# Crossing the quadrants of softmax maxima and sums on VectorE in four more attention units (123 to 126)

## The chip, the cores and the metric

The kernel runs on one core of a Trainium2 chip. The metric is the device time of one execution in microseconds. The core's engines each work through a list of instructions of their own, in order: PE (TensorE, matrix products; PEld is its weight load), DVE (VectorE), ACT (ScalarE), POOL (GpSimd) and SP (SyncE, which here issues most DMAs). They meet only through semaphores. The matrix products write to a memory called PSUM, everything else lies in SBUF; both have 128 partitions, and a quadrant is a group of 32 of them.

## What is computed

A transformer block on 2048 rows of width 576: a layer norm with a shift and scale made from a conditioning vector, attention with 32 query heads over the last 512 rows of a cache of 16 key/value heads, a gated residual, a second layer norm, and a gated MLP of width 4608 with a ReLU on the gate.

```python
W = min(4096, max(256, Sk // 4))                       # 512
q = (x @ wq).reshape(B, Sq, Hq, Dh).transpose(0, 2, 1, 3)
k = jnp.repeat(k_cache[:, :, Sk - W:, :], rep, axis=1)
v = jnp.repeat(v_cache[:, :, Sk - W:, :], rep, axis=1)
p = softmax(einsum("bhqd,bhkd->bhqk", q, k) * Dh ** -0.5)
o = einsum("bhqk,bhkd->bhqd", p, v)
return o.transpose(0, 2, 1, 3).reshape(B, Sq, Hq * Dh) @ wo
...
h = _layernorm(x) * (1 + ca) + sa
x = x + ga * A(h)
h = _layernorm(x) * (1 + cb) + sb
x = x + gb * B(h)                                      # B: (relu(h @ W_gate) * (h @ W_up)) @ W_down
```

## The kernel before

All products take their operands split in two, a rounded high part and the remainder as a low part, and three of the four partial products are summed (high by high, high by low, low by high). So nearly every tile is rounded on ACT (`hi`), and POOL or DVE subtracts to get the rest (`lo`).

Attention runs in 128 units. A unit is one query head on 512 of the 2048 rows; `UNITS` lists them. In unit u the code at the bottom of the listing issues, engine by engine and in this order:

- PE: the scores of u (`s_half` twice, L496 to L498, keys on the partitions, rows along the free axis), the query projection of u+1 (`qproj`, L424), in some units `spread` (L530), a piece of the output projection (`wo_piece`, L660), the first and second half of the product with the values for u-1 (`pv_half`, L633 to L635), another piece. The third product of each score group needs `qlo` of its unit, which DVE made in the unit before (L480).
- DVE: the maximum over the scores in blocks of 32 partitions (L501), the maximum over the four key blocks (`max_pre`), the sums of unit u-1 over blocks of 32 partitions (`sum_pre`, L522), the crossing (below), the broadcast of the maximum (`mb`, L571), the subtraction of the maximum from both halves of the scores (L591), the reciprocal of the sums (L547) and its broadcast (L552), `qlo` of u+1 (L480), the first addition of the key sum (L606), the multiplication of the values' product of u-1 by the reciprocals (L641).
- ACT: the rounding of the query (L476), copies that carry the output projection (L669, L693), the exponentials of the two halves (L593) and their roundings (`hi_half`, L577).
- POOL: two more additions of the key sum (`ksum_op`, L609), then the low parts of both halves (`lo_half`, L600), and the low part of the attention output (L649).

The crossing. After L501 and L522 every partition holds the maximum, or the sum, of its own quadrant; the result over all keys needs the four quadrants together. There are three forms:

- Units 4 to 107, `by_moves`: DVE alone. `cross` copies partitions 64 to 127 beside 0 to 63 and 32 to 63 beside 0 to 31 (`move`, L534, on a small tile), reduces four values to one for maxima and sums (L542), and moves the result back to the other quadrants (L534 twice). Then the reciprocal reads SBUF, later in the unit.
- Units 108 to 126: DVE writes the maxima masked by quadrant (L516), PE multiplies by a matrix of ones and zeros (`spread`, L530, into the PSUM tile `qm`), and DVE reduces what comes back (L558) and takes the reciprocal there and then.
- Units 0 to 3 and 127, `by_pe`: the same crossing through PE, and PE also subtracts the maximum from the scores (L587) with the broadcast maximum that ACT has rounded (`mr`, L569).

`late_hi` is the same test as `by_moves`: where it holds, ACT does both exponentials and then both roundings, otherwise it rounds the first half before the second exponential.

The last units carry work for the MLP besides. Its first matrix product is done with seven products for eight block products, on sums and differences of blocks of the normalized rows. Those are made here: `h0_comb` adds two 128x512 tiles on DVE (L886), `h0_cut` rounds one on ACT (L893) and gets the low part on POOL (L906), or on DVE for 32 partitions of the third tile (L908). A table of times `10 * unit + place` sets where each stands; DVE runs them at the end of a unit, behind L641. L606, L886 and L908 read two tiles in SBUF, L591, L641 and L480 one in PSUM and one in SBUF.

Of the kernel before, what the change touches and what calls it, by code (L numbers as in the profile page):

```python
# [27 lines left out]
CFG = {'a0': (('s', 'vvp', 'vvv'), ('m', 'aap', 'avp'), ('w', 'aav')), 'a1': (('w', 'aap', 'vap'), ('m', 'vvp', 'vvv'), ('s', 'avp'))}  # L28
PE0, PE1, MLP0 = 4, 1, 8
NLAST = 5  # L30
MOVES = 108


@with_exitstack
def kernel(
# [467 lines left out]
                                axis=AX.X, op=ALU.max, apply_transpose=True)  # L503

    def by_moves(u):
        return PE0 <= u < MOVES

    def max_pre(u):
        m = t5[u][:, 0:4, :].rearrange("p k b -> p b k")
        if by_moves(u):  # L510
            nc.vector.tensor_reduce(t5[u][:, 4, :], m, axis=AX.X, op=ALU.max)
            return
        bps[u] = psM.tile([P, 512], F32, tag="mm", name=f"qm{u}")
        t = bps[u][:, 128:144]
        nc.vector.tensor_reduce(t, m, axis=AX.X, op=ALU.max)
        nc.vector.tensor_tensor(t5[u][:, 4:8, :], mask[:, :, None].to_broadcast([P, 4, 16]),  # L516
                                t[:, None, :].to_broadcast([P, 4, 16]), op=ALU.mult)

    def sum_pre(u):
        if u + 1 == NU:  # L520
            t5[NU] = sp.tile([P, 12, 16], F32, tag="t5", name=f"t5_{NU}", bufs=1)
        nc.vector.tensor_reduce(t5[u + 1][:, 5 if by_moves(u + 1) else 8, :],  # L522
                                ks_.pop(u).rearrange("p (b j) -> p b j", j=32),
                                axis=AX.X, op=ALU.add, apply_transpose=True)
# [21 lines left out]
    def sum_inv(u):  # L546
        nc.vector.reciprocal(t5[u + 1][:, 1, :], t5[u + 1][:, 1, :] if by_moves(u + 1) else bps[u + 1][:, 64:80])  # L547
# [1226 lines left out]
```

## Time and profile before

| | us |
|---|---|
| median of 3 runs (2859.11 to 2862.62) | 2862.01 |
| profiled execution | 2857.6 |
| its span | 2855.8 |
| units 108 to 127, from the first score maximum of 108 to the last exponential's input of 127 | 1345.7 to 1588.7 |

The first row counts for comparisons; the breakdown comes from one profiled execution. In the rows of the trace the first number is the start in microseconds from the start of the span, the second the time taken, then engine, line, operation, output and inputs with shapes, and how many instructions were merged. In brackets stands how long the engine had been idle and which engine's instruction released it. A row of merged instructions covers them together. A start to the next start can be a little shorter than the time taken, since an instruction's end overlaps the next one's begin. For the stretches, each row gives start and end, length, busy time of PE, PEld, DVE, ACT and POOL with the number of instructions, the granted TensorE clock as a share of full speed, the share of time the DMA engines were busy, and GB/s.

### The profile page before, as it was taken

To read this page: it belongs to the slowest core of one execution; us is meant where nothing else is said; L and a number is where in the kernel's file an instruction comes from. 1 tells how busy PE (TensorE), PEld (TensorE's weight loads), DVE (VectorE), ACT (ScalarE), POOL (GpSimd) and SP (SyncE) were. 2 spreads that over 40 slices of the span, in tenths; PEclk is the share of its full clock that TensorE was granted. 3 is DMA by queue.
4 is the path that set the end of the run, shared out by engine and by line. 5 is a ranking of instruction groups with operands and counts; after the bars stand their busy time and mean duration, and the time that the engine had idled before them with its cause. 6 is when DMAs were issued, how large, how long until landed. Compare 5 with 4: busy or idle time off the path is not lost.

```text
span 2855.8 us, 41174 instructions
## 1 busy us (share of the span) xinstructions
PE 2815.0 (99%) x15006; PEld 2449.5 (86%) x15006; DVE 2246.8 (79%) x3384; ACT 1476.7 (52%) x2105; POOL 2123.8 (74%) x1564
## 2 busy tenths in 40 slices
PE   6999999999999999999999999999999999999999
PEld 5788888888888888888888888888888888888888
DVE  7899999999889998888889756676677466666666
ACT  5766666666766666666656444444444122222221
POOL 5688888888899989877778766788777356656653
PEclk9999999999999999999999999999999999999999
DMA  4012132222232213312243456666667844444442
GB/s 163 24 45 79 65 106 85 83 82 100 95 104 94 92 62 131 105 70 80 68 155 139 150 213 229 231 240 231 234 234 261 338 165 154 155 155 159 159 154 106
DMA packets 164506, 399.57 MB, mean 140 GB/s; under 512 B 15056, under 2 KB 62160, under 8 KB 164304
## 3 DMA queue, kind: packets, MB, share of 16 engines
q1 hardware_dynamic: 132912, 284.69, 29.9%
q10 hardware_dynamic: 31392, 112.26, 10.0%
q8 instruction: 118, 1.93, 0.3%
q14 instruction: 84, 0.69, 0.1%
HBM read 271.16 MB, written 154.57 MB: 149 GB/s over the span
## 4 chain that ended last, share of the span: by engine, by line
PE 83%; DVE 6%; POOL 5%; issue 2%; ACT 2%; DMA 2%; SPq 0%; ACTq 0%; DVEq 0%; POOLq 0%
PE gu L1016 26%; PE wo L660 12%; PE qps L424 11%; PE md L660 8%; PE st_P L1118 6%; PE s L498 3%; PE s L497 3%; PE s L496 3%; PE pv L635 3%; PE pv L634 3%; PE pv L633 3%; POOL lo L600 2%; DVE t L501 1%; DVE p L591 1%; POOL wop L795 1%
## 5 line engine op out<-in xcount | busy, mean ns | idle before, releaser
L600 POOL TENSOR_TENSOR lo<-p,hi 128x1024 fp32r<-128x1024 f32 x256 | 610.6, 2406 | 1.1 <-ACT hi L577 1.1
L609 POOL TENSOR_TENSOR ks<-ks,p 128x512 f32<-128x512 f32 x256 | 351.7, 1374 | 238.7 <-DVE ks L606 135.5
L501 DVE TRANSPOSE_TENSOR_REDUCE t<-s 128x32 f32<-128x1024 f32 x256 | 313.8, 1239 | 85.9 <-PE s L498 76.6
L1016 PE MATMUL gu<-hop_B,wop 128*128 128x512 f32 x1512 | 375.0, 391 | 0.2 <-POOL wop L795 0.2
L1016 PEld LDWEIGHTS gu<-hop_B,wop 128*128 128x128 f32 x1512 | 274.9, 188 | 51.1 <-POOL wop L795 0.9
L1016 PE MATMUL gu<-hop_T,wop 128*128 128x512 f32 x1260 | 316.1, 391 | 0.0
L424 PE MATMUL qps<-hTa,wA 128*128 128x512 f32 x1288 | 312.9, 394 | 3.1 <-DVE hTa L372 1.6
L660 PE MATMUL wo<-woga,ohi 128*128 128x288 f32 x1472 | 298.8, 295 | 2.0 <-POOL woga L183 1.4
L591 DVE TENSOR_TENSOR p<-s,mb 128x1024 f32<-128x1024 f32 x246 | 290.3, 1219 | 4.2
L424 PEld LDWEIGHTS qps<-hTa,wA 128*128 128x128 f32 x1288 | 244.5, 190 | 56.6 <-DVE hTa L372 3.2
L476 ACT ACTIVATE qhi<-qps 128x512 fp32r<-128x512 f32 x128 | 76.4, 597 | 366.9 <-PE qps L424 358.4
L660 PEld LDWEIGHTS wo<-woga,ohi 128*128 128x128 f32 x1472 | 245.9, 188 | 18.8 <-POOL woga L183 3.4
L1016 PEld LDWEIGHTS gu<-hop_T,wop 128*128 128x128 f32 x1260 | 227.8, 188 | 39.0
L577 ACT CAST hi<-p 128x1024 fp32r<-128x1024 f32 x256 | 259.5, 1042 | 1.5
L660 PE MATMUL md<-wogb,hhi 128*128 128x288 f32 x1272 | 256.9, 295 | 0.4 <-DVE acc L671 0.4
L593 ACT ACTIVATE p<-p 128x1024 f32<-128x1024 f32 x246 | 249.5, 1051 | 13.7 <-DVE p L591 13.4
L671 DVE TENSOR_TENSOR acc<-md,acc 128x576 f32<-128x576 f32 x159 | 119.9, 755 | 160.4 <-PE md L660 159.8
L660 PEld LDWEIGHTS md<-wogb,hhi 128*128 128x128 f32 x1272 | 210.9, 188 | 12.6 <-DVE acc L671 1.4
L1127 DVE TENSOR_TENSOR acc<-st_P,acc 128x576 f32<-128x576 f32 x160 | 121.1, 757 | 127.9 <-PE st_P L1118 127.9
L660 PE MATMUL wo<-woga,olo 128*128 128x288 f32 x736 | 217.8, 296 | 1.3 <-POOL olo L649 1.2
L660 PE MATMUL md<-wogb,hlo 128*128 128x288 f32 x636 | 187.5, 295 | 0.0
L649 POOL TENSOR_TENSOR olo<-rb,ohi 128x512 fp32r<-128x512 f32 x128 | 167.4, 1308 | 15.2 <-ACT ohi L645 15.0
(283 smaller groups left out, 7095.3 us busy)
## 6 DMA issues: line engine op xcount, KB each, us to landing
wop<-wk_P SPq DMA_DIRECT2D x133, 640.0 KB
wk_P<-wop ACTq DMA_DIRECT2D x119, 640.0 KB
wr<-wlay SPq DMA_DIRECT2D x68, 384.0 KB
rogb<-wd SPq DMA_DIRECT2D x68, 288.0 KB
againq<-akq SPq DMA_DIRECT2D x18, 640.0 KB
rwA<-wq SPq DMA_DIRECT2D x32, 320.0 KB
wlay<-wg SPq DMA_DIRECT2D x36, 256.0 KB
roga<-wo SPq DMA_DIRECT2D x32, 288.0 KB
```

The source lines that it names most:

```text
L424: return [lambda i=i, a=a, b=b: nc.tensor.matmul(ps, a, b, start=(i == 0), stop=(i == n - 1)) for i, (a, b) in enumerate(ops)]
L501: nc.vector.tensor_reduce(t5[u][:, 2 * h:2 * h + 2, :].rearrange("p k b -> p (k b)"), t.rearrange("p k (b j) -> p (k b) j", j=32), axis=AX ...
L577: nc.scalar.copy(hi_[u, h], pt[u, h])
L591: nc.vector.tensor_tensor(p, t, bc[u][:, None, :].to_broadcast([P, 2, 512]), op=ALU.subtract)
L593: nc.scalar.activation(p, p, AF.Exp, bias=0.0, scale=1.0)
L600: nc.gpsimd.tensor_sub(lo_[u, h], pt[u, h], hi_[u, h].bitcast(F32))
L609: nc.gpsimd.tensor_tensor(ks_[u], ks_[u], p[:, j, :], op=ALU.add)
L649: nc.gpsimd.tensor_sub(olo[u], o.pop(u), ohi[u].bitcast(F32))
L660: nc.tensor.matmul(ps[:, half, :H2], a[:, sl], w[b][:, cs], start=(n == 0 and seed is None), stop=(n == 5), skip_group_check=seed is not None)
L1016: nc.tensor.matmul(ps, a, c, start=s not in heir(m) and i == 0 and s not in seeds_of(m), stop=i == len(ops) - 1, skip_group_check=True)
L1118: nc.tensor.matmul(ps[:, j, :H2], x[:, sl], w[:, y, :], start=n == 0 and not second, stop=n == 2, skip_group_check=True)
L1127: nc.vector.tensor_tensor(t, ps[:, :, :H2], t, op=ALU.add)
```

## The change

The number that ended the range of units crossed by moves becomes a list of units, and 123 to 126 join it. Unit 122 and those before it down to 108 still cross through PE, and so does 127.

```diff
-MOVES = 108
+MOVES = (*range(4, 108), *range(123, 127))
...
     def by_moves(u):
-        return PE0 <= u < MOVES
+        return u in MOVES
```

DVE's list in unit 123 before, from the maximum over the key blocks to the broadcast of the reciprocals (`t_123` is the small tile of maxima and sums, `qm` the PSUM tile that PE's spread writes):

```order
L515 TENSOR_REDUCE qm_16102<-t_123_16092 128x16
L516 TENSOR_TENSOR t_123_16092<-mask,qm_16102 128x64
L522 TENSOR_REDUCE t_123_16092<-ks_16046 128x16
L558 TENSOR_REDUCE t_123_16092<-qm_16102 128x16
L547 RECIPROCAL t_123_16092<-qm_16102 128x16
L571 STREAM_TRANSPOSE mb_16128<-t_123_16092 128x512
L591 TENSOR_TENSOR p_0_16158<-s_0_16085,mb_16128 128x1024
L591 TENSOR_TENSOR p_1_16163<-s_1_16094,mb_16128 128x1024
L552 STREAM_TRANSPOSE rb_16166<-t_123_16092 128x512
```

The same place in the changed kernel:

```order
L511 TENSOR_REDUCE t_123_16092<-t_123_16092 128x16
L522 TENSOR_REDUCE t_123_16092<-ks_16046 128x16
L534 TENSOR_REDUCE t_123_16092<-t_123_16092 64x32
L534 TENSOR_REDUCE t_123_16092<-t_123_16092 32x64
L542 TENSOR_REDUCE t_123_16092<-t_123_16092 32x16 x2
L534 TENSOR_REDUCE t_123_16092<-t_123_16092 32x32
L534 TENSOR_REDUCE t_123_16092<-t_123_16092 64x32
L571 STREAM_TRANSPOSE mb_16110<-t_123_16092 128x512
L591 TENSOR_TENSOR p_0_16159<-s_0_16085,mb_16110 128x1024
L591 TENSOR_TENSOR p_1_16162<-s_1_16094,mb_16110 128x1024
L547 RECIPROCAL t_123_16092<-t_123_16092 128x16
L552 STREAM_TRANSPOSE rb_16168<-t_123_16092 128x512
```

The mask and the reading back of `qm` are gone, four moves and two reductions have come, and the reciprocal has gone behind the subtractions. On PE the instruction L530 is gone from the place between the query projection and the piece of the output projection, and PSUM's `qm` tile with it; the tiles `qps` and `pv` share two banks in turn, without a third in between.

ACT's list in unit 123 before, from the copy that starts a piece of the output projection to the copy that ends it (`p` is a half of the exponentials, `hi` its rounding):

```order
L693 COPY wo_0_16156<-acc_129 128x2x288
L593 ACTIVATE p_0_16158<-p_0_16158 128x1024
L577 CAST hi_0_16161<-p_0_16158 128x1024
L593 ACTIVATE p_1_16163<-p_1_16163 128x1024
L577 CAST hi_1_16201<-p_1_16163 128x1024
L669 COPY acc_129<-wo_0_16156 128x576
```

And in the changed kernel:

```order
L693 COPY wo_0_16157<-acc_129 128x2x288
L593 ACTIVATE p_0_16159<-p_0_16159 128x1024
L593 ACTIVATE p_1_16162<-p_1_16162 128x1024
L577 CAST hi_0_16165<-p_0_16159 128x1024
L577 CAST hi_1_16203<-p_1_16162 128x1024
L669 COPY acc_129<-wo_0_16157 128x576
```

The second exponential has gone ahead of the first rounding; nothing else moved on ACT. Units 124 to 126 change in the same way. POOL's list and the DMAs of SP keep their order.

## The prediction

> **What bounds the kernel now.** I read the page first, then the stretches of the end of the attention stage, then the instructions of each engine in order of time there.
>
> ```profile
> span 2855.8 us, 41174 instructions
> PE 2815.0 (99%) x15006; PEld 2449.5 (86%) x15006; DVE 2246.8 (79%) x3384; ACT 1476.7 (52%) x2105; POOL 2123.8 (74%) x1564
> PE 83%; DVE 6%; POOL 5%; issue 2%; ACT 2%; DMA 2%; SPq 0%; ACTq 0%; DVEq 0%; POOLq 0%
> ```
>
> Over the whole span PE is the bound. The change touches units 123 to 126 alone, so the stage there counts:
>
> ```profile
> 1297.30:1309.10 11.80, 11.80 (x63) 10.27 (x63) 10.28 (x18) 7.41 (x11) 8.52 (x6) 1.00 0.14 50
> 1533.50:1545.70 12.20, 12.20 (x66) 10.53 (x65) 11.48 (x17) 8.90 (x13) 10.36 (x7) 1.00 0.46 162
> 1545.70:1557.80 12.10, 12.10 (x65) 10.30 (x64) 11.46 (x17) 7.58 (x11) 10.28 (x7) 1.00 0.52 178
> 1582.10:1594.00 11.90, 10.77 (x59) 8.65 (x59) 7.57 (x15) 6.32 (x9) 8.51 (x5) 1.00 0.44 138
> 1590.00:2856.00 1266.00, 1260.99 (x6942) 1111.16 (x6941) 820.51 (x966) 424.47 (x660) 814.44 (x743) 1.00 0.56 199
> ```
>
> Columns: stretch, length, busy time of PE, PEld, DVE, ACT, POOL, then the clock. The first row is a unit that already crosses by moves: DVE has 1.5 us free. The next two are units 123 and 124: DVE is busy 11.5 of 12.1 to 12.2 us, as full as PE. The fourth is unit 127, the fifth everything behind: PE idles 5 us in 1266, so a delay that PE has at 1590 stays.
>
> DVE from the last third of unit 123 to the start of unit 125, with the starts of units 123, 126 and 127 (L501 opens each unit):
>
> ```profile
> 1533.54 2.37 DVE L501 TRANSPOSE_TENSOR_REDUCE t<-s 128x32 f32<-128x1024 f32 x2
> ...
> 1541.55 0.65 DVE L480 SCALAR_TENSOR_TENSOR qlo<-qps,qhi 128x512 fp32r<-128x512 f32 x1
> 1542.12 0.67 DVE L606 TENSOR_TENSOR ks<-p 128x512 f32<-128x512 f32 x1
> ...
> 1543.43 0.68 DVE L908 TENSOR_TENSOR hy_T<-h,hy_T 32x512 fp32r<-32x512 f32 x1
> 1544.14 1.68 DVE L886 TENSOR_TENSOR lfb<-lfb,lfb 128x512 f32<-128x512 f32 x1
> 1545.74 2.37 DVE L501 TRANSPOSE_TENSOR_REDUCE t<-s 128x32 f32<-128x1024 f32 x2
> 1548.14 0.27 DVE L515 TENSOR_REDUCE qm<-t 128x16 f32<-128x64 f32 x1
> ...
> 1549.84 0.23 DVE L558 TENSOR_REDUCE t<-qm 128x16 f32<-128x64 f32 x1 [0.54 <-PE qm L530]
> ...
> 1550.14 0.67 DVE L571 STREAM_TRANSPOSE mb<-t 128x512 f32<-128x512 f32 x1
> ...
> 1554.32 0.67 DVE L606 TENSOR_TENSOR ks<-p 128x512 f32<-128x512 f32 x1
> ...
> 1555.51 0.68 DVE L886 TENSOR_TENSOR lfb<-lfb,lfb 128x512 f32<-128x512 f32 x1
> 1556.11 1.79 DVE L886 TENSOR_TENSOR h<-h,h 128x512 f32<-128x512 f32 x1
> 1557.82 2.37 DVE L501 TRANSPOSE_TENSOR_REDUCE t<-s 128x32 f32<-128x1024 f32 x2
> ...
> 1570.03 2.37 DVE L501 TRANSPOSE_TENSOR_REDUCE t<-s 128x32 f32<-128x1024 f32 x2
> ...
> 1582.11 2.37 DVE L501 TRANSPOSE_TENSOR_REDUCE t<-s 128x32 f32<-128x1024 f32 x2
> ```
>
> No L501 here waits for PE: each follows the instruction before it at once. The only wait is the 0.54 us of the round trip through PE's spread. So DVE's own chain sets when each unit begins, and lengthening it delays the next. The start of 124 lies 12.20 us behind that of 123, the start of 125 12.08 behind that; 12.21 and 12.08 follow.
>
> **The change, part by part.** First the crossing. The price of moves on DVE is in a unit before 108:
>
> ```profile
> 1311.79 0.27 DVE L511 TENSOR_REDUCE t<-t 128x16 f32<-128x64 f32 x1
> ...
> 1314.05 0.71 DVE L571 STREAM_TRANSPOSE mb<-t 128x512 f32<-128x512 f32 x1
> ...
> 1317.07 0.24 DVE L547 RECIPROCAL t<-t 128x16 f32<-128x16 f32 x1
> ...
> 1318.56 0.67 DVE L606 TENSOR_TENSOR ks<-p 128x512 f32<-128x512 f32 x1
> ```
>
> From the first maximum to the broadcast moves take 1314.05 - 1311.79 = 2.26 us; the spread takes 1550.14 - 1548.14 = 2.00, its wait included. From there to the key sum L606 moves take another 4.51, the spread 4.18: the reciprocal now stands alone. Together 6.77 against 6.18, so +0.59 us of DVE per unit, 4 x 0.59 = +2.36. PE loses one spread per unit:
>
> ```profile
> 1549.36 0.44 PE L530 MATMUL qm<-t,quad 128*128 128x80 f32 x2
> 1549.60 0.51 PE L660 MATMUL wo<-againo,ohi 128*128 128x288 f32 x2
> ```
>
> Start to start 0.24 us, four times 0.96. It counts only where PE is the bound.
>
> Second, the exponentials. POOL's two additions to the key sum (L609) need the second exponential and DVE's L606. Rows of POOL in units 123 and 124 (spread) and, last, behind the L606 of 1318.56 (moves):
>
> ```profile
> 1543.76 1.50 POOL L609 TENSOR_TENSOR ks<-ks,p 128x512 f32<-128x512 f32 x1 [1.76 <-ACT p L593]
> 1545.35 1.62 POOL L609 TENSOR_TENSOR ks<-ks,p 128x512 f32<-128x512 f32 x1
> ```
> ```profile
> 1555.95 3.10 POOL L609 TENSOR_TENSOR ks<-ks,p 128x512 f32<-128x512 f32 x2 [1.74 <-ACT p L593]
> ```
> ```profile
> 1319.37 2.65 POOL L609 TENSOR_TENSOR ks<-ks,p 128x512 f32<-128x512 f32 x2 [2.65 <-DVE ks L606]
> ```
>
> Today POOL starts 1.64 and 1.63 us behind L606, held by ACT. With both exponentials first it starts 1319.37 - 1318.56 = 0.81 us behind, held by DVE. That is nothing by itself, but L908 and L886 follow on DVE 1.2 to 1.3 us behind L606, and the rows show that they suffer from POOL. In unit 124 the first L886, begun 0.44 us ahead of POOL, takes 0.60 start to start; the second, begun 0.16 behind POOL's start, takes 1.71. In unit 123 the L886 begun 0.38 behind takes 1.60, L908 ahead of POOL 0.71. The blocked instruction lasts until the POOL instruction ends and some 0.5 us more (1543.76 + 1.50 = 1545.26, and DVE is free at 1545.74, 0.48 later); in return POOL's second addition needs 1.62.
>
> In the changed kernel POOL is 0.8 us nearer, so the first of the pair falls behind POOL's start in every unit and is blocked too, and the second meets POOL's second addition. DVE is then free 0.48 us behind the end of that addition: (1545.35 + 1.62 - 1543.76) + 0.48 = 3.69 us behind POOL's start, so 0.81 + 3.69 = 4.50 behind L606. Now it is 1545.74 - 1542.12 = 3.62 in unit 123 and 1557.82 - 1554.32 = 3.50 in 124; 125 and 126 repeat 123 and 124 in what they run, and in their length (12.21 and 12.08 us). Cost 2 x 0.88 + 2 x 1.00 = +3.76.
>
> The Trainium skill's page "SBUF — State Buffer", section "Who interferes with whom", says that a VectorE instruction with two SBUF inputs and a GpSimd instruction that reads SBUF lock each other out whole, the one that issued second waiting. The trace agrees in kind (0.68 against 1.68 us for the same L886). By that rule alone the blocked instruction would need only the rest of POOL's addition plus its own 0.60; with 2.65 / 2 = 1.33 for an addition I estimate 1.33 - 0.38 + 0.60 = 1.55 where the row has 1.60, which would take 0.2 off the sum. I take the row.
>
> Sum on DVE at the start of unit 127: 2.36 + 3.76 = +6.1 us. Does PE feel all of it? Unit 127 still crosses through PE:
>
> ```profile
> 1586.44 0.23 DVE L558 TENSOR_REDUCE qm<-qm 128x16 f32<-128x64 f32 x1 [0.78 <-PE qm L530]
> ```
> ```profile
> 1587.98 0.62 ACT L569 CAST mr<-mb 128x512 fp32r<-128x512 f32 x1 [5.52 <-DVE mb L566]
> ```
> ```profile
> 1588.66 1.19 PE L587 MATMUL s<-mr,minus 128*128 128x512 f32 x4
> ```
>
> PE's L587 starts 0.06 us behind the end of ACT's cast, which waits for DVE: PE follows DVE there one for one. One thing gives back: L558 waited 0.78 here where the round trip needs 0.54, since PE was the later one; PE will now be early, -0.24. PE's savings of 0.96 and today's idle 1.13 in this unit vanish in the longer wait. So +6.1 - 0.24 = +5.9 us at L587, and nothing behind gives it back. Ahead of it PE stalls on the low part of q:
>
> ```profile
> 1543.90 0.40 PE L498 MATMUL s<-qlo,againk 128*128 128x512 f32 x1
> ```
>
> Its slack is 1543.90 - (1541.55 + 0.65) = 1.70 us. DVE's lag there is 0.59 in unit 123, then 2.06, 3.65 and 5.12, while PE is faster by 0.24 a unit: the slack is gone in unit 124.
>
> The casts of the first half move about 1 us back on ACT; POOL's L600, which reads them, starts only after both additions, so they cost nothing. Queues: no DMA is added, and those that SP issues behind L908's store move by at most the lag, ahead of their use in the next stage.
>
> The profiled execution took 2857.6 us, its span 2855.8; the median of the runs shown is 2862.0, 4.4 above. The difference goes on the median: 2862.0 + 5.9 = 2867.9, which is 0.21%. What a measurement of this kernel can tell from no change is about 0.2%, 5.7 us, so the forecast sits on that border.
>
> **Rivals.**
>
> A, the forecast: both instructions blocked in each unit. With prices off by some 0.6 us and the runs' own scatter it gives 2865.5 to 2870.
>
> B, only one blocked: when the first is done, DVE takes the second ahead of POOL's waiting addition. Then DVE is free 1.98 + 0.60 = 2.58 us behind POOL's start, 3.39 behind L606: 0.23 and 0.11 less than now, -0.68 in four units, and 2.36 - 0.68 - 0.24 = +1.4, so 2863.4. Against it: POOL's second row starts at 1545.35 while the blocked L886 still runs, so it is already in line. It decides at the end of the first blocked instruction.
>
> C, the other side: DVE's lag is swallowed. PE is the bound, saves 0.96, and POOL starts the sums of unit 126 9.99 instead of 10.22 us behind L501, so PE's 1.13 wait shrinks by 0.23: -1.2, 2860.8. It decides at a lag of 1.70 us at qlo; it needs less than 0.4 us per unit, and the crossing alone is 0.59.
>
> D, PE's clock drops in the new gaps. The largest is in unit 127: PE comes to its spread 5.12 - 1.70 = 3.4 us late, DVE's input 6.1 - 0.24 = 5.9 late, so PE idles 2.5. The row of 1582.10 shows clock 1.00 through a gap of 1.13. Only the start of the program shows a lower one:
>
> ```profile
> 0.00:60.00 60.00, 37.80 (x147) 30.11 (x148) 45.23 (x100) 28.01 (x43) 29.75 (x33) 0.94 0.54 193
> ```
>
> There 22 us of idle time cost at most 0.06 x 60 = 3.6 us. As an upper end: +9.5, 2871.5. The Trainium skill's page "TensorE: Matmul & The Clock Gate", Part 1, has the clock halve after an idle window of about 3.4 us; by that rule a gap of 2.5 would be safe and D would not come.
>
> **How the numbers follow.** A 0.80, split by the border 5.7 below its middle of 5.9: 0.48 slower, 0.32 same. D 0.08, slower. B 0.07, same. C 0.05, same but for 0.01 faster by scatter. Slower 0.56, same 0.43, faster 0.01. The range 2863 to 2871 holds A, B and most of D; A's own is 2865.5 to 2870.
>
> **What would show it.** Right: in units 124 to 126 L501 starts 13.7 us apart on DVE; POOL's L609 0.81 us behind L606, released by DVE; L908 and both L886 above 1.2 us; PE waiting for qlo from unit 125 on, and L587 near 1594.6. Wrong: the first of each pair still at 0.7 us (the lock is not what I read), units 12.7 us apart or less, or PE without a wait for qlo (the lag was covered).

## The result, and the profile after

The changed kernel takes 2868.61 us (median of 7 runs, 2863.92 to 2872.21). The kernel before, on the same chip, takes 2859.11 (7 runs, 2855.87 to 2862.62). The ratio is 1.0031 with a 95% interval of 1.0022 to 1.0040: slower by 9.5 us, and between 6.3 and 11.4. The profiled execution took 2863.92 us, the shortest of the seven, and its span stands 6.3 us above that of the kernel before.

The page's head, and the same stretches as were read of before (length, busy time of PE, PEld, DVE, ACT, POOL, then PE's clock, DMA share, GB/s):

```profile
span 2862.1 us, 41170 instructions
...
PE 2814.9 (98%) x14998; PEld 2449.1 (86%) x14998; DVE 2251.5 (79%) x3400; ACT 1477.4 (52%) x2105; POOL 2124.9 (74%) x1564
```
```profile
1560.20:1573.60 13.40, 12.10 (x63) 10.07 (x62) 13.04 (x21) 8.83 (x12) 9.30 (x6) 1.00 0.30 103
...
1587.10:1599.00 11.90, 9.55 (x41) 7.36 (x40) 7.62 (x15) 5.92 (x8) 7.12 (x4) 0.86 0.41 127
```

The first row is unit 125: it now lasts 13.47 us, and PE is busy for only 12.10 of 13.40, since it waits for DVE. The second is unit 127, and there the clock is 0.86, which was 1.00 before. From 1595 to 2862 PE is busy for 1261.86 of 1267.00 us, so it idles 5.1 us there, about as before.

DVE at the start of unit 123, through unit 124 and to the starts of 125 and 127, and POOL's key sum of unit 124 (the idle time before an instruction and what ended it stand in brackets):

```profile
1533.23 2.37 DVE L501 TRANSPOSE_TENSOR_REDUCE t<-s 128x32 f32<-128x1024 f32 x2
...
1555.87 0.67 DVE L606 TENSOR_TENSOR ks<-p 128x512 f32<-128x512 f32 x1
...
1557.07 1.47 DVE L886 TENSOR_TENSOR lfb<-lfb,lfb 128x512 f32<-128x512 f32 x1
1558.46 1.77 DVE L886 TENSOR_TENSOR h<-h,h 128x512 f32<-128x512 f32 x1
1560.15 2.37 DVE L501 TRANSPOSE_TENSOR_REDUCE t<-s 128x32 f32<-128x1024 f32 x2
1562.56 0.26 DVE L511 TENSOR_REDUCE t<-t 128x16 f32<-128x64 f32 x1
...
1569.33 0.67 DVE L606 TENSOR_TENSOR ks<-p 128x512 f32<-128x512 f32 x1
...
1587.08 2.37 DVE L501 TRANSPOSE_TENSOR_REDUCE t<-s 128x32 f32<-128x1024 f32 x2
```
```profile
1556.69 2.99 POOL L609 TENSOR_TENSOR ks<-ks,p 128x512 f32<-128x512 f32 x2 [2.79 <-DVE ks L606]
```

POOL starts 0.82 us behind L606, released by DVE. Both L886 are blocked, 1.39 and 1.69 us from start to start, and DVE is at the next L501 4.28 us behind L606 where it took 3.50 in this unit before.

PE in units 125 and 127, and the first L1016, a product of the MLP:

```profile
1569.46 0.50 PE L498 MATMUL s<-qlo,againk 128*128 128x512 f32 x1 [1.30 <-DVE qlo L480]
...
1590.67 0.45 PE L530 MATMUL qm<-t,quad 128*128 128x80 f32 x2 [1.33 <-DVE t L522]
1591.78 0.73 PE L619 MATMUL pv<-lo,againv 128*128 128x512 f32 x2 [0.16 <-POOL lo L600]
1593.37 2.07 PE L587 MATMUL s<-mr,minus 128*128 128x512 f32 x4 [0.86 <-ACT mr L569]
1597.55 1.77 PE L1016 MATMUL gu<-hop_B,wop 128*128 128x512 f32 x7
```

L587's four products take 2.07 us instead of 1.19. Stretches around them show why; the clock is the third number from the end:

```profile
1590.00:1593.00 3.00, 1.68 (x6) 0.82 (x6) 2.03 (x6) 0.30 (x1) 1.73 (x1) 1.00 0.40 124
1593.00:1594.00 1.00, 0.63 (x2) 0.53 (x3) 0.65 (x1) 1.00 (x3) 0.08 (x1) 0.71 0.78 267
1594.00:1595.00 1.00, 1.00 (x4) 0.81 (x3) 0.07 (x1) 0.69 (x2) 1.00 (x1) 0.50 0.17 65
```

PE ran at half its clock from about 1593.4 to 1596.8, 3.4 us, behind the three small gaps of unit 127.

Where the 6.3 us are, in PE's and DVE's own times: unit 123 began 0.31 earlier (1533.23 against 1533.54), its start to that of unit 127 took 53.85 instead of 48.57 (+5.28), from there to L587 6.29 instead of 6.55 (-0.26), from L587 to the first L1016 4.18 instead of 2.94 (+1.24), and +0.35 behind it. In the kernel before, whose L587 started at 1588.66, that L1016 stands at:

```profile
1591.60 1.77 PE L1016 MATMUL gu<-hop_B,wop 128*128 128x512 f32 x7
```

### The profile page after: what moved, and what is told of

It is laid out like the page before. It is cut to its first block, busy times and chain, and to the rows that moved or that the text cites. A ratio compares the mean times of both kernels' runs of the same rounds, so it can differ in the third digit from the quotient of the medians.

```text
span 2862.1 us, 41170 instructions
## 1 busy us (share of the span) xinstructions
PE 2814.9 (98%) x14998; PEld 2449.1 (86%) x14998; DVE 2251.5 (79%) x3400; ACT 1477.4 (52%) x2105; POOL 2124.9 (74%) x1564
## 5 line engine op out<-in xcount | busy, mean ns | idle before, releaser
L600 POOL TENSOR_TENSOR lo<-p,hi 128x1024 fp32r<-128x1024 f32 x256 | 612.0, 2412 | 1.1 <-ACT hi L577 1.1
L501 DVE TRANSPOSE_TENSOR_REDUCE t<-s 128x32 f32<-128x1024 f32 x256 | 314.0, 1239 | 85.6 <-PE s L498 76.3
L1016 PE MATMUL gu<-hop_B,wop 128*128 128x512 f32 x1512 | 374.7, 391 | 0.2 <-POOL wop L795 0.2
L1016 PEld LDWEIGHTS gu<-hop_B,wop 128*128 128x128 f32 x1512 | 275.0, 188 | 50.7 <-ACT lflh L1001 0.9
L1016 PE MATMUL gu<-hop_T,wop 128*128 128x512 f32 x1260 | 316.1, 391 | 0.0
L1016 PEld LDWEIGHTS gu<-hop_T,wop 128*128 128x128 f32 x1260 | 227.8, 188 | 39.0
L671 DVE TENSOR_TENSOR acc<-md,acc 128x576 f32<-128x576 f32 x159 | 119.9, 755 | 162.8 <-PE md L660 162.1
```

Source lines behind the costliest of these rows:

```text
L501: nc.vector.tensor_reduce(t5[u][:, 2 * h:2 * h + 2, :].rearrange("p k b -> p (k b)"), t.rearrange("p k (b j) -> p (k b) j", j=32), axis=AX ...
L600: nc.gpsimd.tensor_sub(lo_[u, h], pt[u, h], hi_[u, h].bitcast(F32))
L1016: nc.tensor.matmul(ps, a, c, start=s not in heir(m) and i == 0 and s not in seeds_of(m), stop=i == len(ops) - 1, skip_group_check=True)
```

## The experiments

Two explanations of DVE's lengthened units stood at first: that the order of the exponentials brings POOL nearer (the prediction), or that DVE's own lag does. The letters T, R and so on are explained in the expectations where they appear. Times are medians; the kernel before took 2858.74 (23 runs) beside the first four kernels, 2859.48 (15) beside the next, 2858.30 (15) beside the last two. A measure by trace is used with them, since it repeats to 0.1 us: from L501 of unit 123 to L501 of unit 127, and on to PE's L587.

**Moves alone.** The crossing by moves, with the old order of exponentials and roundings:

```diff
 def late_hi(u):
-    return by_moves(u)
+    return by_moves(u) and u < 108
```

> The crossing by moves in units 123 to 126 as in the change, but ACT keeps its old order there (first exponential, first rounding, second exponential, second rounding). Theory T (what blocks is that POOL's key sum waits only for DVE's L606 once DVE is late; the order on ACT no longer matters, because DVE and not ACT is the last): POOL still starts 0.8 us behind L606 in units 124 to 126, units stay near 13.5 us apart on DVE, time within 1 us of the changed kernel, +6 us and more against the kernel before. Rival R (as the prediction had it, the new order on ACT is what brings POOL nearer): POOL starts some 1.6 us behind L606, units are 12.7 us apart, +2 us against the kernel before.

2867.72 us, ratio 1.0032 (1.0021 to 1.0043): the changed kernel again. Its DVE, its POOL and its ACT in unit 124:

```profile
1555.87 0.67 DVE L606 TENSOR_TENSOR ks<-p 128x512 f32<-128x512 f32 x1
...
1557.06 1.46 DVE L886 TENSOR_TENSOR lfb<-lfb,lfb 128x512 f32<-128x512 f32 x1
```
```profile
1556.68 2.99 POOL L609 TENSOR_TENSOR ks<-ks,p 128x512 f32<-128x512 f32 x2 [2.79 <-DVE ks L606]
```
```profile
1553.43 1.06 ACT L593 ACTIVATE p<-p 128x1024 f32<-128x1024 f32 x1 [1.27 <-DVE p L591]
1554.52 1.05 ACT L577 CAST hi<-p 128x1024 fp32r<-128x1024 f32 x1
1555.47 1.05 ACT L593 ACTIVATE p<-p 128x1024 f32<-128x1024 f32 x1
```

ACT rounds between the exponentials, and POOL still starts behind DVE: with the reciprocal and the moves ahead of it L606 ends at 1556.54, no earlier than the second exponential (1556.52).

**Order alone.** The kernel before, with both exponentials first in units 123 to 126 too:

```diff
 def late_hi(u):
-    return by_moves(u)
+    return by_moves(u) or 123 <= u < 127
```

> The kernel before with the crossing through PE everywhere as it was, but both exponentials ahead of both roundings in units 123 to 126. Theory T: with ACT no longer last POOL's key sum starts 0.8 us behind L606, the first of the two SBUF additions behind it on DVE is blocked too, units grow from 12.1 to 13.0 us (about 0.9 each), +3.5 us at unit 127, and the clock may drop behind it for some 1 us more: +3 to +5 us. Rival (only the crossing's 0.59 us per unit and the lost overlap cost): no difference, within 1 us.

2860.59 us, ratio 1.0009 (1.0000 to 1.0018). DVE in unit 124, between the first L501 and the last:

```profile
1531.70 2.37 DVE L501 TRANSPOSE_TENSOR_REDUCE t<-s 128x32 f32<-128x1024 f32 x2
...
1553.14 0.67 DVE L606 TENSOR_TENSOR ks<-p 128x512 f32<-128x512 f32 x1
...
1554.33 1.47 DVE L886 TENSOR_TENSOR lfb<-lfb,lfb 128x512 f32<-128x512 f32 x1
1555.72 1.77 DVE L886 TENSOR_TENSOR h<-h,h 128x512 f32<-128x512 f32 x1
...
1583.15 2.37 DVE L501 TRANSPOSE_TENSOR_REDUCE t<-s 128x32 f32<-128x1024 f32 x2
```

The order alone blocks the first of the pair as well: four units take 51.45 us, +2.88 over before. So either part by itself brings POOL's additions onto DVE's, and doing both costs that once. The changed kernel's 53.85 less 51.45 leaves 2.40 for the crossing. At L587 the order alone is 2.63 us late, and the median rises by 1.9 (0.0 to 5.1).

**The collisions taken away.** The changed kernel, and then the kernel before, with L908 and L886 of units 123 to 126 ahead of L606, when POOL is between instructions:

```diff
-step("h0.a", H + at_, h0_comb, *H0_COMB[key], t)
+step("h0.a", H + at_ - (2.5 if at_ >= 168 else 0), h0_comb, *H0_COMB[key], t)
...
-step("h0.c", H + at_ + (6 if t == 2 else 4 if at_ // 10 % 2 else 6),
+step("h0.c", H + at_ + ((3.5 if at_ >= 162 else 6) if t == 2 else 4 if at_ // 10 % 2 else 6),
...
             q_lo(u + 1)
+        run(u, 5.5)
```

> The changed kernel, with DVE's L908 and L886 of units 123 to 126 moved from the end of the unit to just ahead of L606, when POOL is idle or in its last instruction. Theory T (the port's lock between DVE and POOL costs most of it): L886 takes 0.7 us each, DVE needs 11.7 us per unit, PE is the bound again and has one spread less per unit: units 11.9 us apart, no clock drop in unit 127, -1 us against the kernel before, -7 to -10 against the changed one. Rival (the longer crossing alone keeps DVE the bound): units 12.6 us apart or more, +2 us and more against the kernel before.

> The kernel before, with only the two additions L908 and L886 of units 123 to 126 put just ahead of L606. Theory C (DVE's additions collide with POOL's L609 in the kernel before too): before has a 1.26 and a 1.22 L908 row and first L886 rows near 1.2 in two of the units; ahead of L606, where POOL is between instructions, each should take 0.7 to 0.9, and the units come 1 us closer together over the four: L501(127) some 1 to 2 us earlier, 2856 to 2858 where before stands at 2858.7. Theory M (what was measured of the kernel with moves and sums first, +8.4, comes from the places of these additions): this kernel is slow too, 2864 or more.

On the changed kernel 2867.15 us, ratio 1.0031 (1.0020 to 1.0041); on the kernel before 2860.34, ratio 1.0006 (0.9997 to 1.0014). DVE of the changed kernel with this edit, the starts of units 123, 125 and 127 and an addition of unit 124, and its L587; then the starts of units 123 and 127 and L587 of the kernel before with it:

```profile
1532.09 2.37 DVE L501 TRANSPOSE_TENSOR_REDUCE t<-s 128x32 f32<-128x1024 f32 x2
...
1553.11 0.86 DVE L886 TENSOR_TENSOR lfb<-lfb,lfb 128x512 f32<-128x512 f32 x1
...
1556.41 2.61 DVE L501 TRANSPOSE_TENSOR_REDUCE t<-s 128x32 f32<-128x1024 f32 x2 [0.64 <-PE s L498]
...
1580.07 2.61 DVE L501 TRANSPOSE_TENSOR_REDUCE t<-s 128x32 f32<-128x1024 f32 x2
```
```profile
1587.64 1.09 PE L587 MATMUL s<-mr,minus 128*128 128x512 f32 x4
```
```profile
1532.74 2.37 DVE L501 TRANSPOSE_TENSOR_REDUCE t<-s 128x32 f32<-128x1024 f32 x2
...
1580.65 2.62 DVE L501 TRANSPOSE_TENSOR_REDUCE t<-s 128x32 f32<-128x1024 f32 x2 [0.40 <-PE s L498]
```
```profile
1587.87 1.20 PE L587 MATMUL s<-mr,minus 128*128 128x512 f32 x4
```

No addition takes longer than 0.86 us. In the kernel before with this edit DVE waits for PE at the start of each of units 124 to 127 (0.17 to 0.59 us), which it did in none of them without the edit, and PE is busy for all of the 49 us from 1533 to 1582. In the changed kernel with the edit DVE waits so at unit 125 alone, and PE idles once, 0.71 us, for POOL's L600. The four units take 47.98 with moves and 47.91 without, and L587 comes 55.55 and 55.13 us behind the start of unit 123, where it was 55.12 before. So without collisions PE sets the units of the kernel before, DVE and PE are about even with moves, and the change (its moves, and PE's four spreads fewer) costs next to nothing on the four units and 0.4 us at L587. Taking the collisions out of the kernel before brings nothing: the 0.66 us that DVE gains in the four units it waits for in unit 127. So in the kernel before, DVE with its collisions and PE were about equally long there. Yet the median with moves fell by only 1.5 us, and stands 6.8 above that of the kernel before with the same edit: the collisions explain the stage, not the median. Its profiled run, 2860.75, is the shortest of its seven; the next one is 2866.03. The profiled run's own loss is not in this stage. DVE and POOL in that trace at 1977 us, in the MLP:

```profile
1976.96 6.08 DVE L823 TENSOR_TENSOR wr<-wr,wr 128x768 f32<-128x768 f32 x1
1982.96 0.74 DVE L671 TENSOR_TENSOR acc<-md,acc 128x576 f32<-128x576 f32 x1
```
```profile
1976.88 0.75 POOL L794 TENSOR_TENSOR wop<-wr,wop 32x256 fp32r<-32x256 f32 x1 [1.83 <-ACT wop L793]
1977.61 1.29 POOL L795 TENSOR_TENSOR wop<-wr,wop 128x512 fp32r<-128x512 f32 x1
...
1981.50 0.71 POOL L794 TENSOR_TENSOR wop<-wr,wop 32x256 fp32r<-32x256 f32 x1
1982.19 1.98 POOL L795 TENSOR_TENSOR wop<-wr,wop 128x512 fp32r<-128x512 f32 x1
```

L823 is a sum of two blocks of weights in SBUF (the code calls this one S3). POOL's L794 started 0.08 us ahead of it, and POOL had work in line without a gap (L183 and L1156 stand between the rows shown): the sum ended only during the sixth POOL instruction. The accumulation L671 behind it was late, PE waited 2.4 us for it, and its clock fell again for 3.4 us. Compared with the kernel before, this trace is 3.6 us later behind that place than ahead of it. In the kernel before the same sum started 0.20 us ahead of L794 and took its usual 0.95. So it is a race, and what counts is which of the two starts first:

```profile
1977.77 0.95 DVE L823 TENSOR_TENSOR wr<-wr,wr 128x768 f32<-128x768 f32 x1
```
```profile
1977.97 1.34 POOL L794 TENSOR_TENSOR wop<-wr,wop 32x256 fp32r<-32x256 f32 x1 [1.83 <-ACT wop L793]
```

The kernel before with the sums first lost the same race at 1977.19 (6.07 us), so it is not a matter of the moves alone.

**PE kept busy.** The changed kernel, with four of unit 126's products of the rounded exponentials run twice, in the gap of unit 127; its time holds that extra work:

```diff
+        for kt in range(0 if lows else 2):
+            a = hi_[u, 0][:, kt, :]
+            nc.tensor.matmul(ps, v[:, kt, :], a, start=kt == 0, stop=False, skip_group_check=True)
+            nc.tensor.matmul(ps, v[:, 4 + kt, :], a, start=False, stop=False, skip_group_check=True)
```

> The changed kernel, with four of the eight products of the high part with the values of unit 126 done twice in unit 127 (0.93 us more work on PE, in the 1.3 us in which it waits for DVE there; the first results are overwritten). Theory T (PE's idle time in unit 127 makes the clock drop to half for some 3.4 us): the clock stays at 1.00, PE's L587 takes 1.2 instead of 2.1 us, -1.6 us against the changed kernel in spite of more work. Rival (the clock drop is chance, or needs more to be kept off): no difference, or slower by up to 0.9 us.

2867.74 us, ratio 1.0033 (1.0021 to 1.0044). PE in unit 127 of its trace:

```profile
1592.48 0.45 PE L530 MATMUL qm<-t,quad 128*128 128x80 f32 x2 [0.44 <-DVE t L522]
...
1595.18 1.20 PE L587 MATMUL s<-mr,minus 128*128 128x512 f32 x4 [0.84 <-ACT mr L569]
```

The first gap shrinks from 1.33 to 0.44 us, the other two stay (0.17 and 0.84), the clock stays at 1.00 and L587 takes 1.20 us. That the extra work kept the clock up is not shown by this one profile: in the 3.00 us ahead of L587 PE is busy for 1.69, as much as in the changed kernel (1.68), and among the profiles without the extra work that follow are two (the second of the changed kernel, and that with S3 ahead) in which the clock stayed at 1.00 too. The median shows no gain: this profiled run (2869.28) lost the race of S3 at 2125.72 (7.25 us), PE waited 4.0 us for L671, and, with the MLP's accumulations compared one by one with the kernel before, it lost 5.2 us there.

**Second and third profiles.** The changed kernel twice more, and the one with the sums first once more.

> The changed kernel once more, for a second profile. Theory R: if this run is one of those at .996 or .997 (2866 or more), its trace holds, beside the half-clock stretch at L587 of unit 127, one or two more in the MLP, each behind a DVE sum L823 of 5 us or more that made L671 late and PE wait 2 to 4 us. Theory X: a slow run shows no such row, and its time is lost in small pieces or ahead of unit 123.

> The changed kernel a third time, for the trace of a run at .996 or .997, which neither profile so far is. Theory R: beside the stretch of half clock in unit 127 there are one or two more in the MLP, behind an S3 sum L823 of 6 us or more, and they make up the 3 to 8 us by which it lies above 2863. Theory X: no such sum, the time goes in another place.

> Moves with both sums ahead of L606 once more, profiled: its first profile was its fastest run (2860.75), six others took 2866 to 2872. Theory R: two or three S3 sums of 6 us or more in the MLP, each with 2 to 4 us of waiting for L671 and half a clock behind it; units 123 to 126 again 12.0 apart. Theory P (units 123 to 127 differ from run to run): the MLP is as in the first profile, and L587 of unit 127 comes 5 us or more later than 1587.6.

They took 2862.62, 2870.53 and 2861.54 us. PE's clock in unit 127 of the second profile of the changed kernel, and of the third:

```profile
1590.00:1594.00 4.00, 1.94 (x8) 0.82 (x6) 2.86 (x9) 0.40 (x1) 2.63 (x2) 1.00 0.50 145
1594.00:1595.00 1.00, 0.72 (x3) 0.64 (x4) 0.71 (x1) 1.00 (x3) 0.18 (x1) 1.00 0.72 289
```
```profile
1596.00:1599.00 3.00, 2.53 (x7) 2.16 (x8) 0.87 (x2) 2.65 (x5) 1.27 (x1) 0.50 0.36 118
1599.00:1602.00 3.00, 3.00 (x13) 2.89 (x12) 1.68 (x3) 2.97 (x4) 1.11 (x1) 0.50 0.00 0
```

The four units are the same to 0.05 us in all three (53.85, 53.87, 53.82), and so are the two large gaps of unit 127. The clock was not: no stretch of half clock in one run, one of 3.4 us in another, one of 6.7 us in the third. At the first accumulations of the MLP that is 0, 1.2 and 2.5 us. The third run also began unit 123 2.8 us later than before (its first 100 us have a clock of 0.91, those of before 0.95) and lost the race of S3 at 1917.28, where POOL's L794 had started 0.04 us ahead; this cost 2.0 us. 2.8 at the start, 5.0 in the stage, 2.5 of clock and 2.0 of the race make most of the 12.9 us by which it lies above the profiled run of before. The kernel with the sums first lost the race again, at 1977.82. So in these profiles the stage is fixed, and what differs is the start, the clock in unit 127 and the race.

**S3 moved.** Two ways to take the race out of both kernels. First S3 to POOL, one slot earlier:

```diff
-        nc.vector.tensor_tensor(flat(out), flat(a), flat(b), op=op)
+        (nc.gpsimd if s == "S3" else nc.vector).tensor_tensor(flat(out), flat(a), flat(b), op=op)
...
-        for k, s in {1: [(0, "S1")], 2: [(0, "S4")], 5: [(1, "S3")], 6: [(1, "S2")]}.get(i, []):
+        for k, s in {1: [(0, "S1")], 2: [(0, "S4")], -4: [(1, "S3")], 6: [(1, "S2")]}.get(i, []):
...
+                if i == 4:
+                    sums(m, -4)
```

> The kernel before, with the third of the four sums of weights (S3, 17 instructions L823 of 128x768) given to POOL, in the pause between its L183 and L1156, instead of DVE. Theory R (a race in the MLP: where POOL's L794 starts ahead of DVE's S3 sum, that sum waits 5 us for a gap in POOL's stream, L671 is late, PE waits and its clock falls for 3.4 us): no long S3 sum is left, the runs' times lie closer together (before: 2855.6 to 2861.2), clocks .998 or .999, and the median is 2856 to 2859. Theory X (runs differ for another reason): the same spread as before. If POOL's extra 1.9 us for each sum delays what it splits, PE waits for L795 and the time rises above 2862.

> The changed kernel, with the same move of S3 to POOL. Theory R: the stalls that the profiled run did not have go away in the other runs too; the median falls from 2868.6 to 2862 to 2865, clocks .998 in most runs instead of .996, and it stands 5 to 7 us above the kernel before with S3 on POOL, which is what units 123 to 127 cost in the trace. Theory X: 2867 to 2870 and a spread of 8 us, as the changed kernel.

Then S3 on DVE still, but between L1212 and L1213:

```diff
             nc.vector.tensor_tensor(c, ps, t, op=ALU.add)
+            if m + 1 < NFP:
+                w_sums(m + 1, "S3")
...
-        for k, s in {1: [(0, "S1")], 2: [(0, "S4")], 5: [(1, "S3")], 6: [(1, "S2")]}.get(i, []):
+        for k, s in {1: [(0, "S1")], 2: [(0, "S4")], 5: [(1, "S3")][m > 0:], 6: [(1, "S2")]}.get(i, []):
```

> The kernel before, with the S3 sum (16 of the 17) put one DVE instruction earlier, between L1212 and L1213. Theory R: the S3 sum now starts some 0.7 us earlier, at the end of POOL's L183, and no longer close to L794's start, so none takes 5 us; L1213 and with it POOL's L1156 come about 1 us later, into POOL's pause. Then the runs lie at 2855 to 2858, median 1 to 3 us below the kernel before. If POOL has no room for that 1 us, PE waits for L795 and the time is the same or higher.

> The changed kernel with the same edit. Theory R: 2861 to 2866, median 2863 to 2864 (what is left of the spread are none, one or two half-clock stretches in unit 127 and the start), and 5 to 8 us above the kernel before with the same edit. If the changed kernel's runs lie at 2866 and more for a reason outside the S3 sums, the median stays near 2868.

With S3 on POOL the kernel before takes 2874.01 us (ratio 1.0042, 1.0028 to 1.0055) and the changed one 2880.04 (1.0070, 1.0058 to 1.0083). With S3 ahead they take 2864.48 (1.0017, 1.0008 to 1.0026) and 2868.69 (1.0037, 1.0024 to 1.0051). All are slower than the kernel before. PE's waits in the MLP (line waited for, us in total, times, longest), of the kernel before, with S3 on POOL, and with S3 ahead:

```profile
PE md L660 <- DVE acc L671: 0.4, 1, 0.4
```
```profile
PE md L660 <- DVE acc L671: 8.0, 13, 1.3
PE gu L1016 <- POOL wop L795: 2.6, 8, 1.5
```
```profile
PE md L660 <- DVE acc L671: 2.6, 7, 0.6
```

The one rare long wait went, and many short ones came: on POOL the sums crowd out what DVE needs (L1213 now takes up to 5.56 us), and ahead of L1213 they are blocked by POOL's L795 and L183 in most blocks (up to 3.78 us). As mends both fail. As comparisons they serve, since each has both kernels with the same MLP: the change costs 6.0 us in the one pair and 4.2 in the other.

## Why the prediction was right, and where it was not

The forecast of 2867.9 us, slower, holds against 2868.61. Two errors cancel in that number: it was built on 2862.0, the median of the three runs shown, where the larger samples have 2858 to 2859; and the difference was forecast as 5.9 where the medians have 9.5. That the total came within 0.7 us is luck.

- **Crossing by moves, +0.59 us a unit.** Right: from L511 to L606 6.77 us (1562.56 to 1569.33), as forecast, and 2.40 for four units by the experiment with the order alone, against 2.36. But with the collisions gone the same lag costs only 0.07 us in the four units and 0.4 at L587: it costs its full length because DVE was the bound, and DVE had no slack because of the collisions that it already had.
- **POOL 0.81 us behind L606, released by DVE; both of the pair blocked.** Right: 0.82, by DVE; 1.47 and 1.77 us long in the unit shown. The reason was incomplete. The prediction put it on the exponentials' order alone; the lag does the same without it.
- **The price of the collisions, +3.76.** The step that was mis-sized: 2.88 by the experiment. The 4.50 us from L606 to the next L501 were built from the 3.21 us that POOL's two additions took in unit 123 before; in the changed kernel they take 2.99, so that it is 0.82 + 2.99 + 0.47 = 4.28, and units come 13.46 apart instead of 13.7.
- **-0.24 in unit 127 and PE's stall for qlo from unit 125.** Right: -0.26, L558 waits 0.54, and L498 waits 1.30 us first in unit 125. From L501 of unit 123 to L587 it is +5.02 (60.14 against 55.12) where +5.9 was forecast.
- **Nothing lost behind L587.** The sum had nothing there, and that is wrong: rival D came, which had 0.08. The clock fell in four of the six profiles in which unit 127 was as in the changed kernel (one or two stretches), and in none of the seven profiles of the other kernels that leave PE's products as they were. Its price is smaller than the 3.6 us of the upper end, 1.0 to 1.2 us for one stretch and 2.5 for the double one. The forecast was one gap of 2.5 us; the trace has three, of 1.33, 0.16 and 0.86. The Trainium skill, "TensorE: Matmul & The Clock Gate", Part 1, ties the halving to an idle window of about 3.4 us. Here PE was busy for 1.68 of 3.00 us ahead of it, and never idle for longer than 1.33, so the measurement goes against the reading that such gaps are safe; only the length of the stretch, 3.4 us, is like the page's figure. What decides is open: the second profile of the changed kernel, with 1.69 of 3.00 us and the same gaps, kept its clock.
- **Rivals B and C** did not come: the first of each pair is blocked and so is the second, and no lag was swallowed while the collisions stood.

The stage's +5.0 us and the clock's mean of 1.0 (0, 0, 1.0, 1.2, 1.2 and 2.5 in six profiles) make 6.0 us. The three pairs of kernels have 9.5, 6.0 and 4.2. So the traces come near the last two pairs, and explain of the first all but 0.3 us at the lower end of its interval (6.3 to 11.4), 3.5 in its middle.

The mean granted clock of each run points to where the rest lies, though not to why. Six of the 17 runs of the changed kernel and of the one with moves alone have .998; they took 2862.6 to 2864.9 us, median 2863.5. The kernel before has 25 runs at .998, median 2858.7. That is 4.9 us apart, the stage's price. The other eleven, at .997 and .996, took 2866.1 to 2873.5, while only 14 of the 52 runs of the kernel before have a clock that low, and they took 2859.5 to 2864.1. At equal clock these few are 7 to 8 us apart, so a lower clock alone does not make up the rest. One of the eleven was profiled, the third profile, and beside the stage's 5.0 us it lost time at the start, in a double stretch of half clock and in the race. Whether S3 loses its race more often in the kernels with moves is open. It was seen in five traces out of ten that had S3 in its old place, in kernels with and without moves. The kernel with the sums first stays unexplained in its six other runs: no profile caught one of them. Their clocks, .995 to .997 against .998, would fit two to five more stretches of half clock, and that was not seen.

## What to carry to other kernels

Where two engines hold each other up, as DVE's and POOL's additions of SBUF tiles did here, look not only at how long an engine is busy but at what its neighbour starts just then: 0.6 us of extra work turned one blocked addition per unit into two, and so cost twice its own length. Ask also whether the stage has a second bound close behind: with the collisions gone, the same 0.6 us a unit cost 0.4 us in all at L587. And compare two kernels by a stretch of the trace that repeats (here 48.5 and 53.85 us, to 0.1) before reading much into runs that scatter by 6 us and more. Then check the stretch against the medians all the same: here taking the collisions away mended the stage and left the median where it was but for 1.5 us.

## What the hardware showed that was not expected

PE's clock halved behind gaps of 1.33 us and less, for 3.4 us or twice that, and at the same gaps in another execution not at all. And a DVE sum of 0.95 us took 6.08 when a POOL instruction began 0.04 or 0.08 us ahead of it and others stood in line, but 0.95 when it began 0.20 us ahead of POOL. Behind that line it waited for five POOL instructions. In the attention units it was otherwise: DVE's first blocked addition (1557.07, 1.47 us) ended 1.85 us behind the start of POOL's pair, whose two took 1.30 and 1.62, so it got through behind the first of them. Why one is served next and the other is not, the runs do not show.
